# Combining the mean and variance of four token tiles on Pool, by nine small operations, instead of aggregating them on VectorE

## Chip, cores and metric

One core of one Trainium2 chip. The metric is the device time of one execution in microseconds (us). All runs told here are fast, with a mean granted clock of 0.99 to 1.0. A ratio is the mean time of one kernel's fast runs over the mean time of the other's fast runs of the same rounds, so it is not quite the ratio of the medians that stand beside it. Profiled executions are single ones; their span is 1.7 to 2.2 us shorter than the device time of the same execution.

## The reference, cut to what matters

```python
def _layernorm(x, axis=-1, eps=1e-05):
    m = jnp.mean(x, axis=axis, keepdims=True)
    v = jnp.var(x, axis=axis, keepdims=True)
    return (x - m) / jnp.sqrt(v + eps)
...
    # x: 2048 tokens x 512 channels, bf16
    h = _layernorm(x, axis=-1) * (1 + ca) + sa           # first norm
    x = x + ga * _A_ref(h, A_wqkv, A_wo)                 # windowed attention, 32 heads of 16
    h = _layernorm(x, axis=-1) * (1 + cb) + sb           # second norm
    x = x + gb * _B_ref(h, B_w1, B_b1, B_w2, B_b2)       # starts with a third norm, then mixes tokens
```

Tokens lie on the 128 partitions: 16 tiles of 128x512, handled in four sets of four. Three norms on four sets make twelve groups of statistics; each needs a mean and a reciprocal deviation for each of its four tiles.

## The kernel before

The sums (`bn_stats`) give, for each token, count, mean and sum of squared differences of the even channels and the same for the odd ones; the aggregation (`bn_aggr`) makes mean and variance of them. `ve`, `po`, `ac` and `te` are VectorE, Pool, ScalarE and TensorE. The whole kernel is one list of operations, and a table gives the order in which the engines get them.

```python
def e_stat(e, i):                                  # one tile: VectorE
    ...
    st = small.tile([P, nc.vector.BN_STATS_DIM], F32, name="st", tag=tag + "st")
    ve.bn_stats(out=st[:], in_=tiles(i)[:])
    ve.bn_aggr(out=box[box_key][0][:, i, :], in_=st[:])

def e_rs(e, a, b):                                 # four tiles: Pool (the other groups: ScalarE)
    mv, rs, _ = box[box_key]
    if e == "POOL":
        po.tensor_scalar(out=rs[:, a:b], in0=mv[:, a:b, 1], scalar1=EPS, scalar2=0.0, op0=ALU.add, op1=ALU.add)
        po.tensor_tensor(out=rs[:, a:b], in0=rs[:, a:b], in1=half_t[:, a:b], op=ALU.pow)
        return
    ...

def normalize(e, dst, src, key, i):                # xn or hb: waits for rs
    mv, rs, nm = box[key]
    if e == "DVE":
        ve.tensor_scalar(out=dst, in0=src, scalar1=mv[:, i, 0:1], scalar2=rs[:, i : i + 1], op0=ALU.subtract, op1=ALU.mult)
    else:
        po.tensor_scalar(out=dst, in0=src, scalar1=nm[:, i : i + 1], scalar2=rs[:, i : i + 1], op0=ALU.add, op1=ALU.mult)
```

(Cuts are marked by "...".) After the second norm comes `h = xn * bc`, `h = h + bc`, and the third norm makes `hb` of `h`. Beside the norms, ScalarE takes the exponentials of the attention (`et<-psa`, 75 of them of 128x1536), VectorE multiplies some of them by a mask (`et<-et,maskt`) and copies TensorE's results out of PSUM. (`QT`, `kb` and `VT` are queries, keys and values, `psa` and `psb` the scores in PSUM, `pxy` the products of exponentials and values, `pu` the products behind the third norm.)

The softmax here doesn't subtract the row's maximum and nothing guards it: scores larger than these inputs give would overflow.

Of the kernel before, what the change touches and what calls it, by code (L numbers as in the profile page):

```python
# [10 lines left out]
ALU = mybir.AluOpType  # L11
# [38 lines left out]
128 197 199 129D 328P 130A 99D 200 125D 154 71 126D 153 329D 201 110 72 73 207 111A 112D 208 113 74 198 115D 114D  # L50
202 181 182 203 155 183D 156 204 215 185 209 205 162 86 29 157D 216 163 789 30 206 210 165D 178 211 179 217 164D 223
212 166 224 213 184 167 180D 158 169D 159 168A 214 160D 218 225 161D 189 219 76 230 79 220 173 231 190 221 174 77
222 226 191D 175D 192 170 227 549 171 232 177 234 176 228 172D 186 235 187 193 229 194 330D 233 331D 332D 238 236
333D 334 188D 239 335 338 337D 339 237 336D 340D 246 240 341D 345 247 550 355 346 78 250 248 347D 356 251 349 241
357D 365 366 242 257 367D 252 389 258 790 350 390 243 261 259 244 351 262 245 352D 249 253 391D 265 254 551 392 263
373 266 75 359 374 87 370 375D 371 255 273 372D 267 342 274 552 381 382 256 343 383D 275 277 344D 385 260 278 264
348 360 268 358 279 395 361 396 353 287 362D 376 288 269 289 399 368 397 284 791 400 377 285 386 286 553P 387 270
403 401 271 792 364 272 404 276 369 280 388D 296 281 363 412 405 378 282 354 290 413 283 379 393 398 380D 394 554P
416 414 555P 297 402 417 384 406 291 556D 293 407 557D 423 418 292 558P 294 408 424 559 409 411 560 295 410 415 561D
425 428 298 419 429 562D 563 564 606 566D 420 432 565D 430 299 607 433 585 301D 300P 586 608D 421 587D 440 434 614  # L60
422 441 595 302D 596 303P 445 442 427 426 304D 793P 446 615 431 616D 452 447 597D 618 435 453 570 305P 571 444 436
306D 456 1034 454 572D 307P 1033 598 457 603 599 617 437 461 308P 458 438 604 314 462 309P 439 443 600D 448 605D 463
469 310P 449 590 470 591 580 311P 592D 450 473 589 471 451 581 315 474 460 455 573 459 312D 594 582D 481 475 567
794D 482 610 568 609 464 569D 465 485 316 602 483 575 486 593 611 576 601 466 489 487 583 467 577D 490 468 472 588
476 584 477 498 478 574 612 491 479 619 1032 613D 499 484 488 795D 313D 492 796P 317 493 502 500 509 480 797P 503
510 512 318P 513 494 620 504 495 798P 319D 621 496 511 501 321P 505 521 322P 506 626 514 622 518 507 320D 625 515
627 323P 508 516 623 497 578 522 631 628 579 519 517 632 520 624 629 640 633 523 799 641 803 800 804 524 634 645 642
525P 630 646 805D 635 526D 801D 527P 636 802D 653 647 806D 807 654 643 808 528D 810 809D 811 529P 637 658 655 812D
815 659 638 820 530D 816 648 531D 663 660 817D 639 664 644 661 649 532D 539 843 650 672 665 656 844 651 533D 673 821
652 534P 657 822D 666 677 674 662 678 535P 845D 854 540 667 668 536P 685 679 541 855 686 851 819 856D 852 537D 838  # L70
669 853D 538P 687 690 670 839 691 835 840D 836 675 695 692 680 671 688 696 676 693 681 837D 830 682 542 704 697 846
683 847 543P 705 684 831 698 689 544D 709 706 832D 547P 694 710 825 548D 813 699 848D 826 700 545D 717 711 546P 827D
1039 718 1040 707 1044 823 1041 701 722 712 719 1042 858 702 723 1045 1043D 841 703 708 814 727 724 1050 857 728 713
842 1046 714 736 833 729 1047 737 1051 828 1048D 1049 1052 859 1036 725 1053 715 818 741 1054D 738 752 742 720 753
849 716 749 721 730 743 860 824 726 754 861 731 744 1055 850 750 732 865 862 834 751 1056 866 1057 761 829 1061 1062
739 733 870 867 734 1058 762 871 735 1060 740 1059D 1035 745 1038 872 879 1063 746 873 880 1066 1067 868 1064 747
884 1065D 881 1068 748 885 1069 882 758 1071 1070D 759 1037 863 892 886 760 755 893 756 864 757 869 894 763 874 897
875 1072 898 764 1073 1074 895 765P 1077 887 876 899 902 877 1075 766D 903 767P 1078 1076D 878 768D 911 904 900 883
912 769D 888 770D 1079 771D 1083 889 772D 913 779 916 1084 917 1085 905 1086 1080 773D 890 918 924 1082 891 925 896
919 1081D 901 906 774D 914 907 929 1088 908 926 1089 909 775D 930 910 927 915 776P 780 920 921 934 777D 931 1087D  # L80
1090 778P 935 1091 781 1094 1095 1092D 922 943 782 936 988 944 1096 923 783P 1097 937 928 945 932 948 989 949 1098D
933 784D 990 938 787P 991 939 1000 950 786P 956 992 940 788P 957 1099 993 1100 785P 941 1101 1002 1102 1001 958 961
1104 1103D 1116 962 951 1117 1008 1119 946 1120 1003 1009 966 1118 963 942 947 967 1010 952 1121 1122 964 953 1105
1011 968 975 1012 954 1106 969 976 1123 1107 959 1108 955 1124 977 980 960 981 978 965 1109D 970 1125 1013 971 1110
1020 972 1126 982 973 1111 1021 983 974 1127 979 984 1022 994 985 1158 1172 1028 1112 986 1167 1113 1023 1093 987
1164 995 1029 1114A 1159 996 997 1160 998 1171 1004 1162 1128 1163 1129 999 1161 1005 1177 1115 1130 1131 1166 1132
1014 1168 1006 1134 1165 1189 1170 1015 1181 1007 1169 1133 1135 1016 1137 1136 1138 1017 1173 1139 1140 1201 1018
1024 1141 1185 1019 1143 1025 1026 1144 1142 1027 1030 1146 1031 1147 1145 1174 1178 1175 1190 1193 1176 1179 1205
1148 1180 1182 1186 1183 1202 1206 1187 1149 1188 1191 1194 1150 1184 1209 1192 1213 1195 1210 1151 1196 1197 1198
1152 1199 1153 1221 1200 1154 1222 1203 1155 1217 1204 1207 1156 1214 1157 1249 1211 1239 1240 1215 1259 1225 1216  # L90
1241 1208 1218 1229 1212 1219 1230 1260 1223 1242 1269 1231 1226 1261 1227 1232 1250 1228 1233 1224 1243 1279 1220
1299 1262 1234 1244 1289 1263 1251 1280 1252 1300 1253 1290 1254 1301 1255 1281 1235 1245 1236 1302 1282 1246 1283
1291 1256 1264 1247 1319 1309 1237 1284 1270 1238 1285 1271 1310 1292 1320 1311 1293 1312 1303 1272 1321 1322 1273
1265 1329 1266 1304 1274 1257 1275 1323 1276 1339 1313 1286 1330 1267 1349 1294 1268 1324 1258 1350 1248 1331 1332
1333 1325 1295 1340 1277 1341 1359 1296 1278 1334 1305 1297 1314 1287 1298 1360 1361 1306 1288 1315 1362 1316 1369
1351 1326 1335 1363 1317 1352 1327 1364 1342 1307 1343 1353 1336 1308 1370 1318 1344 1328 1345 1371 1346 1354 1379
1337 1355 1347 1372 1380 1356 1348 1365 1338 1373 1357 1374 1366 1358 1375 1381 1376 1382 1383 1377 1384 1367 1385
1386 1368 1378 1387 1388
# [55 lines left out]
def kernel(  # L154
# [357 lines left out]
    def norm_ops(tag, tiles, deps, poss, box_key, parts, pool=True):  # L512
        st_ops, rs_of = [], {}

# [9 lines left out]
        def e_stat(e, i):  # L524
            if i == 0:
                box[box_key] = (
                    small.tile([P, 4, nc.vector.BN_AGGR_DIM], F32, name="mv", tag=tag + "mv"),
                    small.tile([P, 4], F32, name="rs", tag=tag + "rs"),
                    small.tile([P, 4], F32, name="nm", tag=tag + "nm"),
                )  # L530
            st = small.tile([P, nc.vector.BN_STATS_DIM], F32, name="st", tag=tag + "st")
            ve.bn_stats(out=st[:], in_=tiles(i)[:])
            ve.bn_aggr(out=box[box_key][0][:, i, :], in_=st[:])

        def e_rs(e, a, b):
            mv, rs, _ = box[box_key]
            if e == "POOL":
                po.tensor_scalar(out=rs[:, a:b], in0=mv[:, a:b, 1], scalar1=EPS, scalar2=0.0, op0=ALU.add, op1=ALU.add)
                po.tensor_tensor(out=rs[:, a:b], in0=rs[:, a:b], in1=half_t[:, a:b], op=ALU.pow)
                return  # L540
            ac.activation(out=rs[:, a:b], in_=mv[:, a:b, 1], func=ACT.Ln, bias=eps_t[:], scale=1.0)
            ac.activation(out=rs[:, a:b], in_=rs[:, a:b], func=ACT.Exp, scale=-0.5)

        for i in range(4):
            prev = [st_ops[-1]] if st_ops else []
            st_ops.append(op(f"{tag}st", {"DVE": 0.82}, lambda e, i=i: e_stat(e, i), deps=deps[i] + prev, pos=poss[i]))
            for a, b in parts:
                if b == i + 1:
                    o = op(f"{tag}rs", {"ACT": 0.46, "POOL": 0.6 + 0.145 * (b - a)} if pool and tag != "l1" or b - a == 4 else {"ACT": 0.46}, lambda e, a=a, b=b: e_rs(e, a, b), deps=st_ops[:], pos=poss[i])
# [717 lines left out]
```

## Time and profile before

| | before |
|---|---|
| time, median (lowest to highest) | 267.67 us (267.42 to 267.75), 3 runs |
| span of the profiled execution | 265.2 us |
| ScalarE idle from 100 to 130 us | 0.06 us |
| first of the last long run of matmuls | 199.5 us |

The prediction below shows the lines that carry the reading. In the lines in the order in time come the start, the length, then the instruction; an idle time ahead of it stands in brackets. These three are the first instructions on VectorE that need the statistics of the groups at 107, 126 and 155 us:

```profile
110.03 0.41 DVE L194 TENSOR_TENSOR h<-xn,bc_all 128x512 bf16<-128x512 bf16 x1
...
128.47 0.57 DVE L194 TENSOR_SCALAR hb<-h,mv,rs 128x512 bf16<-128x512 bf16 x1
...
157.55 0.42 DVE L194 TENSOR_TENSOR h<-xn,bc_all 128x512 bf16<-128x512 bf16 x1
```

And this is the chain that ended last, by engine:

```profile
PE 67%; ACT 19%; DVE 8%; issue 4%; POOL 0%; ACTq 0%; POOLq 0%
```

Pool has no share in it.

### The profile page before, as it was taken

The numbers are of one execution on the slowest core, as the hardware profiler recorded it, in microseconds if no ns is written. First come the engines' busy times: TensorE is split into PE (matmuls) and PEld (weight loads), VectorE is DVE, ScalarE is ACT, GpSimd is POOL, SyncE is SP. The second block draws the span as 40 slices with busy tenths as digits, with TensorE's granted clock in tenths as the row PEclk, the third lists the DMA queues.
The fourth block names the chain that finished last, engine by engine and source line by source line (L and its number), as shares of the span: only waits on it lengthen the run. The fifth ranks groups of instructions, "written<-read, shape, count | busy, mean of one in ns | idle before, by whom it ended". The sixth has DMA issues, their size and how long they took to land.

```text
span 265.2 us, 10676 instructions
## 1 busy us (share of the span) xinstructions
PE 248.8 (94%) x4769; PEld 136.8 (52%) x4769; DVE 195.5 (74%) x444; ACT 185.4 (70%) x268; POOL 91.1 (34%) x153
## 2 busy tenths in 40 slices
PE   7898999999989888899999999999999999999993
PEld 2575666656656654455544454445444444444441
DVE  7768896777847559999948888999998730415875
ACT  2479999999999899999999999999416432000000
POOL 8054321495289946543893031440000000000000
PEclk9999999999999999999999999999999999999999
DMA  6996400000018000000015872011499800001122
GB/s 205 362 381 206 47 5 4 5 2 5 2 31 213 5 4 5 0 5 2 4 27 136 220 184 79 5 44 40 143 373 397 355 4 0 20 0 63 59 99 79
DMA packets 31598, 25.34 MB, mean 96 GB/s; under 512 B 6076, under 2 KB 29632, under 8 KB 31552
## 3 DMA queue, kind: packets, MB, share of 16 engines
q1 hardware_dynamic: 31544, 24.66, 29.5%
q8 instruction: 37, 0.61, 0.9%
q14 instruction: 9, 0.07, 0.1%
q10 hardware_dynamic: 8, 0.00, 0.0%
HBM read 22.55 MB, written 2.10 MB: 93 GB/s over the span
## 4 chain that ended last, share of the span: by engine, by line
PE 67%; ACT 19%; DVE 8%; issue 4%; POOL 0%; ACTq 0%; POOLq 0%
PE pu L194 32%; ACT et L194 16%; PE pxy L194 13%; PE psa L194 8%; PE pq L194 5%; PE pa L194 4%; PE pv L194 3%; ACT lz L194 3%; DVE st L194 2%; DVE VT L194 1%; PE pt L194 1%; DVE part L194 1%; PE psb L194 1%; DVE h L194 1%; DVE mv L194 0%
## 5 line engine op out<-in xcount | busy, mean ns | idle before, releaser
L194 ACT ACTIVATE et<-psa 128x1536 bf16<-128x1536 f32 x75 | 109.2, 1455 | 4.0 <-PE psa L194 1.9
L194 PE MATMUL pu<-hb,w1p 128*128 128x512 bf16 x224 | 53.2, 380 | 0.7 <-DVE part L194 0.7
L194 PE MATMUL pu<-guT,w 128*128 128x512 bf16 x224 | 49.0, 379 | 0.0
L194 ACT ACTIVATE et<-psb 128x512 bf16<-128x512 f32 x75 | 45.1, 601 | 0.0
L194 PE MATMUL pxy<-et,ones_bd 128*32 128x192 bf16 (+3 forms) x960 | 38.7, 233 | 0.7 <-issue 0.7
L194 PE MATMUL pxy<-et,VT 128*32 128x192 bf16 (+3 forms) x960 | 38.4, 234 | 0.9 <-DVE OT L194 0.5
L194 PEld LDWEIGHTS <-w 128*128 128x128 bf16 x224 | 21.9, 98 | 26.4
L194 PE MATMUL psa<-QT,KT 32*128 32x192 bf16 (+3 forms) x720 | 30.0, 230 | 5.6 <-ACT et L194 4.9
L194 POOL TENSOR_SCALAR KT<-kb,mask_par 128x512 bf16<-128x512 bf16 (+1 forms) x36 | 22.9, 645 | 31.0 <-DVE kb L194 22.3
L194 PEld LDWEIGHTS <-w1p 128*128 128x128 bf16 x224 | 20.2, 98 | 25.6 <-issue 2.3
L194 PE MATMUL pq<-h1T,wqkv 128*128 128x512 bf16 (+1 forms) x128 | 30.1, 355 | 0.3 <-ACT VT L194 0.3
L194 PEld LDWEIGHTS <-KT 32*128 32x128 bf16 x960 | 16.2, 92 | 26.4 <-issue 24.1
L194 PEld LDWEIGHTS <-VT 128*32 128x32 bf16 x960 | 23.6, 96 | 11.6 <-issue 10.1
L194 PE MATMUL psb<-QT,KT 32*128 32x192 bf16 (+3 forms) x240 | 29.4, 231 | 0.0
L194 DVE SCALAR_TENSOR_TENSOR o<-pu,b2FM,bc_all 128x512 f32<-128x512 f32 x16 | 11.6, 748 | 20.2 <-PE pu L194 20.1
L194 DVE TENSOR_TENSOR et<-et,maskt 128x512 bf16<-128x512 bf16 (+2 forms) x56 | 24.9, 480 | 0.6 <-ACT et L194 0.5
L194 PEld LDWEIGHTS <-ones_bd 128*32 128x32 bf16 x960 | 23.2, 97 | 1.0 <-issue 0.9
L194 DVE BATCH_NORM_STATS2 st<-x 128x6 f32<-128x512 bf16 x32 | 21.8, 680 | 0.2
L194 DVE TENSOR_TENSOR OT<-pxy,lz 128x256 bf16<-128x256 f32 x32 | 13.4, 419 | 10.6 <-ACT lz L194 10.1
L194 PEld LDWEIGHTS <-wqkv 128*128 128x128 bf16 x192 | 14.0, 97 | 13.4 <-issue 4.8
L194 PE MATMUL pv<-wqkv,h1T 128*32 128x256 bf16 x512 | 17.9, 274 | 0.2 <-DVE VT L194 0.2
L194 PE MATMUL pa<-wod,OT 128*128 128x512 bf16 x64 | 17.3, 381 | 0.3 <-ACT part L194 0.3
(113 smaller groups left out, 355.1 us busy)
## 6 DMA issues: line engine op xcount, KB each, us to landing
w1p<-in_B_w_dram SPq DMA_DIRECT2D x14, 512.0 KB, 6.3
w<-in_B_w_dram SPq DMA_DIRECT2D x14, 512.0 KB, 8.3
wmod<-in_w_mod_dram SPq DMA_DIRECT2D x6, 512.0 KB, 5.5
x<-in_A_x_dram SPq DMA_DIRECT2D x16, 128.0 KB, 4.6
out_dram<-otile SPq DMA_DIRECT2D x16, 128.0 KB, 1.7
wqkv<-in_A_wqkv_dram SPq DMA_DIRECT2D x2, 384.0 KB, 5.5
wqkv<-in_A_wqkv_dram SPq DMA_DIRECT2D x1, 512.0 KB, 5.3
wod<-in_A_wo_dram SPq DMA_DIRECT2D x1, 512.0 KB, 8.7
```

What stands on the lines that cost most here:

```text
L194: ins = call(*args, **kwargs)
```

## The change

The intent: VectorE is busy for 74% of the span and Pool for 34%, so Pool is to make mean and variance of four tiles at once, and VectorE keeps the sums only. It applies to nine of the twelve groups. The epsilon and the negated mean are folded into the nine operations, and the power follows. In the order of instructions each chain takes the place that the negated mean had.

```diff
 def e_stat(e, i):
+    if quad:                                       # the nine groups
+        if i == 0:
+            box[box_key, "st"] = small.tile([P, 4, nc.vector.BN_STATS_DIM], F32, name="st4", ...)
+        ve.bn_stats(out=box[box_key, "st"][:, i, :], in_=tiles(i)[:])
+        return
     st = small.tile(...)
     ve.bn_stats(out=st[:], in_=tiles(i)[:])
     ve.bn_aggr(out=box[box_key][0][:, i, :], in_=st[:])
+
+def e_agg(e):
+    t = small.tile([P, 4, 2], F32, name="agg", ...)
+    po.tensor_tensor(out=t[:, :, 0], in0=st[:, :, 1], in1=st[:, :, 4], op=ALU.subtract)
+    po.tensor_tensor(out=t[:, :, 1], in0=st[:, :, 1], in1=st[:, :, 4], op=ALU.add)
+    po.tensor_tensor(out=t[:, :, 0], in0=t[:, :, 0], in1=t[:, :, 0], op=ALU.mult)
+    po.tensor_scalar(out=mv[:, :, 0], in0=t[:, :, 1], scalar1=0.5, ...)
+    po.tensor_scalar(out=nm[:], in0=t[:, :, 1], scalar1=-0.5, ...)
+    po.tensor_scalar(out=t[:, :, 0], in0=t[:, :, 0], scalar1=0.25, scalar2=EPS, op0=ALU.mult, op1=ALU.add)
+    po.tensor_tensor(out=t[:, :, 1], in0=st[:, :, 2], in1=st[:, :, 5], op=ALU.add)
+    po.tensor_scalar(out=t[:, :, 1], in0=t[:, :, 1], scalar1=1.0 / D, ...)
+    po.tensor_tensor(out=mv[:, :, 1], in0=t[:, :, 0], in1=t[:, :, 1], op=ALU.add)

 def e_rs(e, a, b):
-    if e == "POOL":
-        po.tensor_scalar(out=rs[:, a:b], in0=mv[:, a:b, 1], scalar1=EPS, ...)
-        po.tensor_tensor(out=rs[:, a:b], in0=rs[:, a:b], in1=half_t[:, a:b], op=ALU.pow)
+    if quad:
+        po.tensor_tensor(out=rs[:], in0=mv[:, :, 1], in1=half_t[:], op=ALU.pow)
         return
```

## The prediction

> **What bounds the kernel now.** I read the page's busy shares first, then a table of busy time by stretch, then the groups that the change touches, then the order in time on Pool, VectorE and TensorE.
>
> ```profile
> PE 248.8 (94%) x4769; PEld 136.8 (52%) x4769; DVE 195.5 (74%) x444; ACT 185.4 (70%) x268; POOL 91.1 (34%) x153
> ```
>
> VectorE at 74% and Pool at 34% make the move look right: take from the busier, give to the idler. But 74% is a mean. By stretch (columns: stretch, its length, then the busy time of PE, PEld, DVE, ACT, POOL):
>
> ```profile
> 80.00:100.00 20.00, 18.10 (x647) 12.56 (x638) 12.13 (x27) 18.86 (x26) 15.97 (x25) 1.00 0.26 66
> 100.00:110.00 10.00, 7.75 (x169) 4.29 (x158) 9.84 (x24) 9.96 (x14) 6.07 (x10) 1.00 0.01 3
> 110.00:120.00 10.00, 9.47 (x269) 5.61 (x268) 9.68 (x23) 9.99 (x15) 5.07 (x5) 1.00 0.01 3
> 130.00:150.00 20.00, 20.00 (x379) 9.35 (x376) 14.19 (x29) 19.70 (x28) 11.49 (x15) 1.00 0.33 90
> 150.00:170.00 20.00, 19.43 (x425) 10.30 (x423) 17.91 (x45) 19.35 (x27) 4.27 (x5) 1.00 0.50 125
> 170.00:185.00 15.00, 15.00 (x305) 7.46 (x304) 14.24 (x35) 14.53 (x22) 4.90 (x6) 1.00 0.14 38
> 200.00:265.00 65.00, 60.96 (x283) 27.43 (x281) 33.71 (x52) 10.51 (x15) 0.00 (x0) 1.00 0.27 103
> ```
>
> From 100 to 120 us ScalarE (the exponentials) is busy 19.95 of 20 us and VectorE 19.52. From 130 TensorE is full, to 185 with ScalarE close behind; the last 65 us are TensorE alone. The chain that ended last says the same: PE 67%, ACT 19%, DVE 8%. So VectorE is nearly full from 100 to 130 and from 160 to 200, but beside another full engine. A shorter VectorE shortens the kernel only where a full engine waits for it, and those waits are small: from 40 to 185 us ScalarE's whole idle time is 4.2 us.
>
> **What the Trainium skill says.** "Perfetto Trace Analysis", section "Optimizing Scalar/DVE Operations": a VectorE instruction on SBUF has about 60 ns of access overhead that occupies the engine, its profiled latency being about twice that. The trace agrees in kind: the aggregation shows 182 ns, yet the next instruction starts 0.10 us after it. The section also warns that moving work between VectorE and Pool may not help as they share a port. "SBUF — State Buffer", section "SBUF: two separate sides": that shared pair is an exclusive lock, held for a whole instruction, against Pool's reads, by VectorE instructions in a two-port mode or with two SBUF inputs. The mask multiply has two SBUF inputs, and the trace agrees: a Pool scalar operation on 128x4 takes 0.23 to 0.24 us alone and 0.85 beside a mask multiply. "GPSIMD Engine Reference", section "Instruction dispatch": each Pool instruction passes a sequencer and a software dispatcher, so small size doesn't make it cheap; here 128x4 takes about what a 64x64 copy takes (233 ns).
>
> **The change part by part.** It touches nine of the twelve groups of statistics (three norms on four sets of tiles); the first set of the first norm and the last set of the other two keep the old way.
>
> ```profile
> L194 DVE BATCH_NORM_AGGREGATE mv<-st 128x2 f32<-128x6 f32 x48 | 8.7, 182 | 1.7
> L194 DVE SCALAR_TENSOR_TENSOR nm<-mv 128x4 f32<-128x4 f32 x8 | 1.4, 180 | 0.1
> L194 POOL TENSOR_SCALAR rs<-mv 128x4 f32<-128x4 f32 x9 | 3.0, 337 | 32.5 <-DVE mv L194 32.4
> L194 POOL TENSOR_TENSOR rs<-rs,half_t 128x4 f32<-128x4 f32 x9 | 9.9, 1104 | 0.8
> ```
>
> VectorE loses 36 of 48 aggregations and the eight 128x4 negated means. An aggregation costs its slot: sums plus aggregation take 0.82 us start to start (49.58 to 50.40), a copy of the sums' duration 0.61 (50.84 to 51.45), so about 0.21. 36 x 0.21 + 8 x 0.09 = 8.3 us of slots, about 8 us off the busy time of 195.5.
>
> Pool gains nine small operations per group and loses the addition of epsilon and the one negated mean it had. At 0.235 us: 81 x 0.235 - 3.0 - 0.2 = +15.8, so Pool's busy time goes to about 107 us (40%), somewhat more with lock waits.
>
> The latency is what matters. In the built program seven of the ten operations wait for one before them on Pool. Such a pair costs 0.33 us start to start (56.29 to 56.62), operations that do not wait 0.20 (eight copies in 1.56). Two at 0.20 and seven at 0.33 give 2.7, plus the power of 1.03: 3.7 us from the last sum to the reciprocal deviation, against 0.33 + 1.03 = 1.36 now. The aggregation off VectorE gives 0.2 back: about 2.1 us later per group, 3 where mask multiplies hold the lock. Order: each chain now stands where the negated mean stood; nothing else in the order of PE, ACT or the queues changes. On VectorE later instructions that need the statistics then block what stands behind them.
>
> Pool, VectorE and TensorE around the two groups that matter most:
>
> ```profile
> 106.81 0.85 POOL L194 TENSOR_SCALAR rs<-mv 128x4 f32<-128x4 f32 x1 [2.87 <-DVE mv L194]
> 107.74 1.03 POOL L194 TENSOR_TENSOR rs<-rs,half_t 128x4 f32<-128x4 f32 x1
> 108.88 0.76 POOL L194 TENSOR_SCALAR xn<-x,nm,rs 128x512 bf16<-128x512 bf16 x1
> ...
> 170.24 0.23 POOL L194 TENSOR_SCALAR rs<-mv 128x4 f32<-128x4 f32 x1 [1.66 <-DVE mv L194]
> 170.56 1.65 POOL L194 TENSOR_TENSOR rs<-rs,half_t 128x4 f32<-128x4 f32 x1
> 172.71 3.02 POOL L194 TENSOR_SCALAR hb<-h,nm,rs 128x512 bf16<-128x512 bf16 x4 [0.50 <-DVE nm L194]
> ```
>
> ```profile
> 110.03 0.41 DVE L194 TENSOR_TENSOR h<-xn,bc_all 128x512 bf16<-128x512 bf16 x1
> ```
>
> ```profile
> 174.47 1.89 PE L194 MATMUL pu<-hb,w1p 128*128 128x512 bf16 x8
> 176.63 1.90 PE L194 MATMUL pu<-hb,w1p 128*128 128x512 bf16 x8
> ```
>
> Group by group, in time:
> - 20 us: the first consumer is at 34.8. Nothing.
> - 61 us: normalized tiles about 2 us later, transposes at 65.5 and 67.9. Just fits.
> - 70 us: VectorE's normalize at 72.06 waits until about 73.4; the copies behind it come some 0.5 us later. Cost 0 to 0.5.
> - 74 us: moves to about 86, into Pool's stretch without a gap (75.6 to 93.4), and delays keys, values and the small copies that free exponential buffers by 3.5 to 4 us. The first exponential of the next group of tiles starts at 98.84; those are ready at 95 to 96.5. Just fits.
> - 97 us: statistics at 101.5 instead of 98.3; VectorE's first `hb` (101.11) stalls about 1 us. Cost 0 to 1.
> - 107 us: beside mask multiplies, so 3.7 to 4.3 us; Pool's normalize ends near 111, while VectorE wants it (the row at 110.03) and would by then be there a little earlier. A stall of 1 to 2 us with ScalarE and VectorE both full. Cost 0.5 to 1.
> - 126 us: `hb` of the sixth tile on Pool goes from 130.45 to about 132; its first matmul is the eighth from 130.27, at 131.8. Cost 0.3 to 0.8, TensorE being full.
> - 155 us: VectorE stalls about 1.5 us at 157.55 in front of mask multiplies. Cost 0.3 to 1.
> - 170 us: Pool makes all four `hb`, the last at 175.7; the matmuls at 176.63 start with that last one. Spare 0.9, delay 0.2 to 1.2 after VectorE's own gain of 0.6. Cost 0 to 0.5.
>
> Sum of costs 1.1 to 4.8, middle about 2.5. Against it stands VectorE's gain: of 8.3 us most falls in gaps or beside full engines. I give it 1 to 1.5 us, for matmuls and exponentials that now wait for an evacuation or a mask. Net about +1.2, so 268.9 us.
>
> **Rivals.**
> (1) VectorE is a real bound from 100 to 130 and from 160 to 200; its 8 us count in part, and the time falls by 1 to 3 us (265 to 266.5). For it: 98% busy from 100 to 110. Against it: ScalarE at 99.6% there, TensorE at 100% from 170 to 185, and the last 10 us before the final matmuls (189.7 to 199.5), the one VectorE-led stretch of the chain, holds only tiles that the change leaves alone.
> (2) Pool's chains stall VectorE's queue at five places; the stalls spread, since TensorE runs in order and the score banks leave it about 0.2 us per chunk before ScalarE waits. All 4.8 us and the locks: 272 to 274. For it: Pool was without a gap from 75.6 to 93.4. Against it: six exponential buffers and TensorE's idle 2.25 us from 100 to 110.
> (3) All delays are absorbed and nothing gained: 267.5, the same.
>
> **Range and chances.** My middle is between (2) and (3): 268.9, range 266.4 to 272.2. Two per cent is 5.35 us: below 262.3 nothing in the trace leads, as ScalarE's and TensorE's work is unchanged: 0.03. Above 273.0 needs rival (2) almost whole: 0.10. The rest, 0.87, within 2%.
>
> **What would show it.** Right, if in the changed profile VectorE's busy time is 187 to 188, Pool's 105 to 110, each chain from first small operation to the end of the power is 3.5 to 4.5 us, VectorE shows new waits for Pool near 72, 101, 110 and 157 of 0.5 to 2 us, and the final matmuls start 0 to 3 us later than 199.5. Wrong, if these matmuls start before 198.5 (VectorE was a bound), or if ScalarE's idle time between 100 and 130 goes from 0.1 to over 3 us (stalls spread), or if a small Pool operation takes over 0.4 us on average.

## The result and the profile after

| | before | after |
|---|---|---|
| time, median (lowest to highest) | 267.71 us (267.42 to 268.0), 4 runs | 271.09 us (270.64 to 271.44), 4 runs |
| ratio, 95% interval | | 1.0125 (1.0107 to 1.0144) |
| span of the profiled execution | 265.2 us | 268.9 us |
| first of the last long run of matmuls | 199.5 us | 203.2 us |

The kernel is slower by 3.4 us. That lies in the predicted range of 266.4 to 272.2, but the loss is nearly three times the +1.2 us that the prediction gave.

The busy times on the page after:

```profile
PE 244.9 (91%) x4727; PEld 136.8 (51%) x4769; DVE 189.7 (71%) x400; ACT 185.8 (69%) x268; POOL 105.8 (39%) x224
...
PE 56%; DVE 14%; POOL 12%; ACT 11%; issue 5%; POOLq 0%; ACTq 0%
```

VectorE lost 5.8 us and Pool gained 14.7, as planned, and the chain that ended last (the second line) now goes over Pool for 12%, where it had 0%. (42 matmul records are missing in this trace, x4727 for x4769, so TensorE's busy time can't be compared to a per cent.) Pool's new work, from the groups of instructions (count, then busy time and mean ns, then idle time before and what ended it):

```profile
L193 POOL TENSOR_TENSOR rs<-mv,half_t 128x4 f32<-128x4 f32 x9 | 9.4, 1050 | 0.7
L193 POOL TENSOR_TENSOR agg<-st 128x4 f32<-128x4 f32 x27 | 6.0, 240 | 24.7 <-DVE st L193 24.0
L193 POOL TENSOR_SCALAR agg<-agg 128x4 f32<-128x4 f32 x18 | 4.2, 232 | 1.5
```

The same stretches as in the prediction (busy time of PE, PEld, DVE, ACT and POOL, then the granted clock, the DMA share and GB/s):

```profile
100.00:110.00 10.00, 6.95 (x157) 3.93 (x156) 9.06 (x19) 9.29 (x14) 7.73 (x18) 1.00 0.01 3
110.00:120.00 10.00, 8.54 (x238) 5.16 (x241) 8.25 (x19) 9.17 (x12) 5.18 (x5) 1.00 0.01 3
130.00:150.00 20.00, 18.63 (x420) 9.52 (x414) 12.96 (x26) 18.48 (x26) 14.92 (x19) 1.00 0.22 59
150.00:170.00 20.00, 18.36 (x389) 9.77 (x394) 16.06 (x37) 18.59 (x25) 4.69 (x12) 1.00 0.59 156
170.00:185.00 15.00, 14.14 (x276) 6.96 (x271) 13.81 (x32) 14.59 (x24) 7.77 (x15) 1.00 0.13 37
```

ScalarE, which was busy for 19.95 of the 20 us from 100 to 120, is now busy for 18.46; from 130 to 150 it has lost 1.2 us. No engine is full any more: the engines wait for each other. Pool around the group at 107 us shows how:

```profile
106.63 1.00 POOL L193 TENSOR_TENSOR agg<-st 128x4 f32<-128x4 f32 x2 [1.75 <-DVE st L193]
107.58 0.20 POOL L193 TENSOR_TENSOR agg<-agg 128x4 f32<-128x4 f32 x1
...
108.75 0.20 POOL L193 TENSOR_SCALAR agg<-agg 128x4 f32<-128x4 f32 x1
109.03 0.20 POOL L193 TENSOR_TENSOR mv<-agg 128x4 f32<-128x4 f32 x1
109.31 1.31 POOL L193 TENSOR_TENSOR rs<-mv,half_t 128x4 f32<-128x4 f32 x1
110.73 0.77 POOL L193 TENSOR_SCALAR xn<-x,nm,rs 128x512 bf16<-128x512 bf16 x1
```

One small operation that waits for the one before it comes 0.28 us after it (108.75, 109.03) and takes 0.20. The chain from the first operation to the end of the power takes 3.99 us here (106.63 to 110.62), where the kernel before took 1.96 (106.81 to 108.77, in the prediction's lines). Where no mask multiply is near it takes 3.06 (the groups at 20 and 97 us). On VectorE, the three instructions of the last section are now these:

```profile
111.53 0.42 DVE L193 TENSOR_TENSOR h<-xn,bc_all 128x512 bf16<-128x512 bf16 x1 [1.78 <-POOL xn L193]
...
131.17 0.41 DVE L193 TENSOR_SCALAR hb<-h,mv,rs 128x512 bf16<-128x512 bf16 x1 [1.44 <-POOL rs L193]
...
161.61 0.42 DVE L193 TENSOR_TENSOR h<-xn,bc_all 128x512 bf16<-128x512 bf16 x1 [1.39 <-POOL xn L193]
```

All three wait for Pool. Behind each of them stand copies that TensorE needs, and behind TensorE stand the exponentials:

```profile
104.93 0.29 PE L193 MATMUL pxy<-et,VT 128*32 128x256 bf16 x4 [1.01 <-POOL VT L193]
112.61 1.66 PE L193 MATMUL pv<-wqkv,h1T 128*32 128x256 bf16 x48 [0.90 <-DVE QT L193]
132.24 1.73 PE L193 MATMUL pu<-hb,w1p 128*128 128x512 bf16 x6 [0.65 <-DVE kb L193]
```

```profile
114.65 1.45 ACT L193 ACTIVATE et<-psa 128x1536 bf16<-128x1536 f32 x1 [0.83 <-PE psa L193]
```

This suggests a ruler for all that follows: number the 75 exponentials of 128x1536, and take the start of each in the changed kernel minus its start in the kernel before. This *slip* grows only where time is lost. For the changed kernel it is -0.26 at the first (17.7 us), -0.25 at the 35th (96.7 us) and +3.70 at the last (183.6 us), and it grows in six steps. I number the nine groups by their time in the kernel before: 1 at 20 us, 2 at 61, 3 at 70, 4 at 74 (moved to 86), 5 at 97, 6 at 107, 7 at 126, 8 at 155, 9 at 170.

| step of the slip | near | follows from | size, us |
|---|---|---|---|
| groups 1, 2, 3 | to 80 us | | 0 |
| groups 4 and 5 | 105 us | TensorE waits for Pool's values (`VT`, started at 103.52 for 102.60) | 0.67 |
| group 6 | 113 us | VectorE's `h` waits for Pool | 0.82 |
| group 7 | 132 us | VectorE's `hb` waits for Pool | 1.09 |
| group 7, second step | 141 us | | 0.25 |
| group 8 | 165 us | VectorE's `h` waits for Pool | 0.83 |
| group 9 | 179 to 181 us | TensorE waits for Pool's `hb` | 0.29 |
| sum from the 35th exponential on | | | 3.95 |

The ruler has an error that has nothing to do with the change. The slip of the first exponential differs from profile to profile by up to 2.2 us (it is 0.33 us in one kernel below that is as fast as the kernel before). TensorE also has pauses that the profile puts down to "issue", near 87 us (0.70 us before, 1.03 after) and sometimes near 159 us, and they too differ from profile to profile. So I read steps at the groups, not the slip as a whole. The step of 0.67 us at groups 4 and 5 came only with both of them changed: with groups 1 to 4 alone, and with 5, 7 and 9 alone (both below), no step stands near 105 us.

### The profile page after: what moved, and what is told of

Its sections match the earlier page's. It is cut to its first block, busy times and chain, and to the rows that moved or that the text cites. A ratio compares the mean times of both kernels' runs of the same rounds, so it can differ in the third digit from the quotient of the medians.

```text
span 268.9 us, 10666 instructions
## 1 busy us (share of the span) xinstructions
PE 244.9 (91%) x4727; PEld 136.8 (51%) x4769; DVE 189.7 (71%) x400; ACT 185.8 (69%) x268; POOL 105.8 (39%) x224
## 4 chain that ended last, share of the span: by engine, by line
PE 56%; DVE 14%; POOL 12%; ACT 11%; issue 5%; POOLq 0%; ACTq 0%
PE pu L193 29%; ACT et L193 9%; PE pxy L193 7%; PE psa L193 6%; PE pq L193 6%; PE pv L193 4%; DVE st L193 3%; POOL agg L193 3%; PE pa L193 2%; DVE et L193 2%; POOL rs L193 2%; ACT lz L193 2%; POOL hb L193 2%; DVE h L193 1%; DVE part L193 1%
## 5 line engine op out<-in xcount | busy, mean ns | idle before, releaser
L193 PE MATMUL pu<-hb,w1p 128*128 128x512 bf16 x212 | 51.8, 380 | 2.6 <-DVE kb L193 0.7
L193 PEld LDWEIGHTS <-KT 32*128 32x128 bf16 x960 | 15.6, 92 | 25.8 <-issue 23.8
L193 PE MATMUL pq<-h1T,wqkv 128*128 128x512 bf16 (+1 forms) x112 | 27.4, 350 | 1.4 <-issue 0.8
L193 POOL TENSOR_SCALAR VT<-vn,half_m 128x512 bf16<-128x512 bf16 x24 | 17.8, 755 | 0.0
```

What stands on the lines that cost most here:

```text
L193: ins = call(*args, **kwargs)
```

## The experiments

The theory: the loss is how late the reciprocal deviations come, which the engines pass on one to one where nothing hides it; the work taken off VectorE earns nothing by itself. Rivals: (a) the load on Pool and on the port that it shares with VectorE slows both; (b) the new place in the order of instructions costs; (c) VectorE's relief earns its few microseconds and hides an even larger loss.

### Relief without lateness, lateness without relief, order, a shorter chain

**Relief alone.** The kernel before, with the aggregations dropped from the nine groups; mean and variance are read from the even channels' sums. The statistics are wrong, though the result was still within the tolerance.

```diff
-    ve.bn_aggr(out=box[box_key][0][:, i, :], in_=st[:])
+    # nine groups: mv is the view st[:, :, 1:3] (mean and squares of the even channels)
-    po.tensor_scalar(out=rs, in0=mv[..1], scalar1=EPS, scalar2=0.0, op0=ALU.add, op1=ALU.add)
+    po.tensor_scalar(out=rs, in0=mv[..1], scalar1=2.0 / D, scalar2=EPS, op0=ALU.mult, op1=ALU.add)
```

> The kernel before with the 36 aggregations simply left out of VectorE (the mean and spread are read from the even half alone, so the result is wrong on purpose); Pool does what it did before, in the order of before. Theory 'late statistics' (the loss comes from statistics that arrive later, VectorE's relief is worth little): 266.9 to 267.6, final matmuls at most 0.5 to 0.8 us earlier. Rival 'VectorE is a bound in two stretches': 263 to 265.5.

Measured: 268.28 us beside 267.13, ratio 1.0041 (1.0023 to 1.006): slower than the 266.9 to 267.6 expected, and far from the rival's 263 to 265.5. VectorE's busy time fell to 190.5 us and the reciprocal deviations came 0.11 to 0.45 us earlier, and nothing was gained: from the 35th exponential on no step of the slip is below -0.01 us. The small loss consists of 0.57 us ahead of the first exponential, of pauses of TensorE by "issue" (1.30 us near 87, 0.52 near 160) and of 0.33 us near 119. There VectorE's mask multiply took 1.81 us in place of 0.95, and TensorE waited 0.48 us for it. It had started (118.09) behind a Pool multiply of 1.16 us that was running (117.93). In the kernel before VectorE was first (117.21, Pool 117.25), and Pool's multiply took 1.93 us. So which of the two comes first decides who loses there.

**Lateness without relief.** The changed kernel, with the 36 aggregations put back on VectorE, into tiles that nobody reads.

```diff
     ve.bn_stats(out=box[box_key, "st"][:, i, :], in_=tiles(i)[:])
+    spare = small.tile([P, nc.vector.BN_AGGR_DIM], F32, name="spare", tag="spare")
+    ve.bn_aggr(out=spare[:], in_=box[box_key, "st"][:, i, :])
     return
```

> The kernel after with the 36 aggregations kept on VectorE as well, their results unread: the Pool chains without the relief. Late statistics: 271.3 to 272.3, because the relief showed only as 0.4 us of earlier exponentials before 80 us. Rival 'VectorE is a bound': 273 or more, as the relief then hid part of the delay.

Measured: 273.02 us beside 267.13, ratio 1.0238 (1.0211 to 1.0264). The theory's 271.3 to 272.3 failed, and the rival's 273 or more came true: beside late chains the relief is worth 2.5 us by the medians (5.9 lost here, 3.4 by the changed kernel, on different chips). From the 35th exponential on the steps sum to 4.5 us here and to 3.95 in the changed kernel, so only 0.55 of the 2.5 us can be placed at the groups. The two profiled executions differ by 1.8 us, and 1.2 of it lies ahead of 88 us. Of that, 0.37 is there at the first `pq` matmul (9.85 us for 9.48), ahead of the first aggregation put back (15.74), and 0.35 is a wait of TensorE for the DMA of a weight near 14 us, so these are not the aggregations' doing. What makes up the rest of the 2.5 us stays open, and rival (c) is not out by this run.

**Order alone.** The kernel before, with its two Pool operations moved to where the changed kernel has its chain.

```diff
-... 301D 300P ...        # reciprocal deviation ahead of its old place
+... 301D ... 300P ...    # at the place that the changed kernel gives it, nine times
```

> The kernel before, with only the place of Pool's two operations (epsilon, power) moved behind the negated mean, as in the kernel after. Late statistics: 267.4 to 268.3, the same as before. Rival 'the place in the order': most of the loss, 269.5 to 271.

Measured: 267.29 us beside 267.13, ratio 1.0001 (0.9981 to 1.0021). Rival (b) is out.

**Six operations for nine.** Correct too: the sums are added pairwise in one operation of 128x8, the negated mean is made of that, and VectorE's normalize adds it.

```diff
-    (nine operations)
+    po.tensor_tensor(out=t[:], in0=st[:, :, 1:3], in1=st[:, :, 4:6], op=ALU.add)
+    po.tensor_scalar(out=nm[:], in0=t[:, :, 0], scalar1=-0.5, ...)
+    po.tensor_scalar(out=t[:, :, 1], in0=t[:, :, 1], scalar1=1.0 / D, scalar2=EPS, ...)
+    po.tensor_tensor(out=t[:, :, 0], in0=st[:, :, 1], in1=nm[:], op=ALU.add)
+    po.tensor_tensor(out=t[:, :, 0], in0=t[:, :, 0], in1=t[:, :, 0], op=ALU.mult)
+    po.tensor_tensor(out=mv[:, :, 1], in0=t[:, :, 0], in1=t[:, :, 1], op=ALU.add)
```

> The kernel after with six small operations in place of nine (both sums in one operation, half the difference as even mean plus negated mean, the mean read by VectorE as the negated mean): right result. Chain without lock waits about 2.2 us in place of 3.06. Late statistics: a loss about in proportion to the time over the 1.36 us of before, so 268.8 to 269.8; rival 'place in the order' or a loss that only one large wait makes: 270.5 to 271.

Measured: 269.01 us beside 267.13, ratio 1.0069 (1.0053 to 1.0086). As expected: three operations fewer take back about half of the loss.

### Which groups

The changed kernel's code in some groups and the old code in the others:

```diff
-quad = parts == [(0, 4)]
+quad = parts == [(0, 4)] and box_key in QUADS     # groups 1 to 4; 5, 7 and 9; 6 and 8
```

> The change in the first four groups only (20, 61, 70 and 74 us), the other five as before. In the trace of the kernel after, the exponentials slip by no more than about 0.3 us against before until the fifth group. Late statistics: 267.0 to 267.8. Rival 'Pool backlog' (the fourth chain, moved into the stretch without a gap, delays keys and values of the next tiles): 0.7 us or more of loss, 267.8 to 268.8.

> The change in groups five, seven and nine only (97, 126 and 170 us: the third norm). From the slips of the exponentials in the kernel after (0.67 at 104, 1.1 at 133, 0.3 at 180) late statistics gives +2.1, less where the fifth no longer meets the backlog of the fourth: 268.4 to 269.4. Rival 'only the order or the sum counts': a third of the loss, 268.2.

> The change in groups six and eight only (107 and 155 us: second norm, VectorE waits for Pool's normalized tile). Slips in the kernel after 0.82 and 0.83: late statistics 268.4 to 269.1. Rival: two ninths of the loss, 267.9.

Measured, beside 266.98 us:

| groups changed | median | ratio, 95% interval | steps of the slip |
|---|---|---|---|
| 1 to 4 | 267.45 us | 1.0013 (0.9999 to 1.0027) | none at the groups |
| 5, 7, 9 | 269.66 us | 1.0095 (1.0079 to 1.0111) | group 7: 1.53 and 0.25; group 9: 0.34 |
| 6, 8 | 269.54 us | 1.0092 (1.0078 to 1.0105) | group 6: 1.28; group 8: 1.17 |

The first four groups are free, as expected. (The second kernel has two more steps of 0.3 us: near 96, where TensorE had paused by "issue" for 0.33 us, and near 119, where the mask multiply took 1.81 us as under "Relief alone".) The other two sets cost somewhat more than expected, and together more than all nine at once: group 6 steps by 1.28 us here and by 0.82 in the changed kernel. There 0.67 us were already lost at groups 4 and 5, and lateness counts from what is lost already.

### Load or lateness

**Fillers ahead of the wait, in all groups.** The kernel before, and ahead of each addition of epsilon seven small operations in a chain that nobody reads. Pool carries the load, and in its idle time, if it has any there.

```diff
+    fill = small.tile([P, 4, 2], F32, name="fill", ...)
+    po.tensor_tensor(out=fill[:, :, 0], in0=half_t[:], in1=half_t[:], op=ALU.add)
+    for n in range(6):
+        po.tensor_scalar(out=fill[:, :, (n + 1) % 2], in0=fill[:, :, n % 2], scalar1=0.5, scalar2=0.0, op0=ALU.mult, op1=ALU.add)
     po.tensor_scalar(out=rs[:, a:b], in0=mv[:, a:b, 1], scalar1=EPS, ...)
     po.tensor_tensor(out=rs[:, a:b], in0=rs[:, a:b], in1=half_t[:, a:b], op=ALU.pow)
```

> The kernel before with seven small dependent operations that nobody reads put on Pool in front of each of the nine additions of epsilon. They need nothing from VectorE, so where Pool would have idled for the statistics they run in the idle time: nearly the load of the kernel after on Pool and on the shared port, without later statistics. Late statistics: 267.0 to 268.0 (the fourth group, in Pool's stretch without a gap, may cost up to 0.8). Rivals 'Pool's load' and 'port contention': 269 to 271.

Measured: 269.58 us beside 266.98, ratio 1.0098 (1.008 to 1.0115). The expectation failed, and by itself this looks like rival (a). But the slip is 2.94 us by the 31st exponential (87.6 us) and 2.95 at the 52nd (132.6 us): the fillers of groups 5 and 6 and the first step of group 7 cost nothing (0.55 us near 141 us is all that follows), and the loss lies ahead of them, at groups 1 to 4. Not all of it need be the fillers': in this profile TensorE's granted clock was 0.50 from 81.4 to 84.8 us, where it was 1.0 in the kernel before. Up to 1.7 us of the 2.94 (half of these 3.4, an estimate) can be that. At groups 1, 2 and 4 Pool does not wait ahead of the addition (at group 3 it waits 6.59 us). In the kernel before, around group 4:

```profile
73.80 0.46 POOL L194 TENSOR_SCALAR rs<-mv 128x4 f32<-128x4 f32 x1
...
76.33 0.76 POOL L194 TENSOR_SCALAR xn<-x,nm,rs 128x512 bf16<-128x512 bf16 x1
```

and with the fillers:

```profile
75.34 1.58 POOL L194 TENSOR_SCALAR fill<-fill 128x4 f32<-128x4 f32 x6
76.99 0.24 POOL L194 TENSOR_SCALAR rs<-mv 128x4 f32<-128x4 f32 x1
...
79.02 0.77 POOL L194 TENSOR_SCALAR xn<-x,nm,rs 128x512 bf16<-128x512 bf16 x1
```

No idle time stands ahead of the addition there, so the fillers made the statistics late, and with them everything behind them on Pool, which the experiment was meant not to do; load and lateness can't be told apart in these groups. (The changed kernel avoids that, since it moves this chain to 86 us.) So the next pair was made for groups 5 to 9 only.

**The same fillers ahead of the wait, or behind it.** In the first kernel the seven operations stand ahead of the addition of epsilon, in the second between it and the power. The two kernels have the same instructions.

```diff
-                (all groups)
+                if box_key in LATE:          # groups 5 to 9
                     fill ... seven operations, ahead of the addition
```

> Groups 5 to 9 only: seven small operations that nobody reads, in a chain, on Pool ahead of the addition of epsilon, where Pool waits for the sums anyway. Pool carries the load of the change, its port use is there, but no statistic is later by more than a few tenths. Theory (the loss is how late the statistics are): within 0.4 us of the kernel before, 266.7 to 267.4. Rival (Pool's load and the shared port slow VectorE): 268 to 269.5, with mask multiplies slower than before. The earlier run with fillers in all groups lost 2.4 us ahead of 90 us; if the theory holds that part is gone here.

```diff
                 po.tensor_scalar(out=rs[:, a:b], in0=mv[:, a:b, 1], scalar1=EPS, ...)
+                if box_key in LATE:
+                    fill ... the same seven operations
                 po.tensor_tensor(out=rs[:, a:b], in0=rs[:, a:b], in1=half_t[:, a:b], op=ALU.pow)
```

> The same seven operations in the same five groups, but between the addition of epsilon and the power, so that every reciprocal deviation comes about 1.8 us later (more beside mask multiplies). VectorE keeps its aggregations. Theory: the loss of the changed kernel without its relief, 269.8 to 271.5, with new stalls at exponentials 42, 51 and 66. Rival (load): the same as the run with the operations ahead of the addition.

Measured, beside 267.06 us on one chip: ahead 267.13 us, ratio 1.0002 (0.9982 to 1.0022); behind 272.97 us, ratio 1.0214 (1.0193 to 1.0234). On VectorE, the three instructions with the fillers ahead:

```profile
110.06 0.41 DVE L196 TENSOR_TENSOR h<-xn,bc_all 128x512 bf16<-128x512 bf16 x1
...
128.49 0.58 DVE L196 TENSOR_SCALAR hb<-h,mv,rs 128x512 bf16<-128x512 bf16 x1
...
157.82 0.43 DVE L196 TENSOR_TENSOR h<-xn,bc_all 128x512 bf16<-128x512 bf16 x1 [0.17 <-POOL xn L196]
```

and with the same fillers behind:

```profile
111.93 0.43 DVE L196 TENSOR_TENSOR h<-xn,bc_all 128x512 bf16<-128x512 bf16 x1 [1.95 <-POOL xn L196]
...
131.97 0.41 DVE L196 TENSOR_SCALAR hb<-h,mv,rs 128x512 bf16<-128x512 bf16 x1 [1.78 <-POOL rs L196]
...
162.71 0.43 DVE L196 TENSOR_TENSOR h<-xn,bc_all 128x512 bf16<-128x512 bf16 x1 [1.75 <-POOL xn L196]
```

Pool's busy time is 99.0 us in the one and 99.3 in the other, both 8 above the kernel before. In the first every step of the slip from the 35th exponential on is 0.02 us or less; in the second they sum to 5.5 us. In these groups the load costs nothing that the runs can show (the interval ends at 1.0022), and the lateness costs all. Rival (a) is out here, by the cleanest pair. The second kernel lost more than I expected (269.8 to 271.5): I had sized it from the changed kernel, whose chains in groups 6 to 8 are less late (table below).

**A chain shorter than before.** The addition of epsilon is dropped, so the power reads the variance (the result stays within tolerance).

```diff
-    po.tensor_scalar(out=rs[:, a:b], in0=mv[:, a:b, 1], scalar1=EPS, scalar2=0.0, op0=ALU.add, op1=ALU.add)
-    po.tensor_tensor(out=rs[:, a:b], in0=rs[:, a:b], in1=half_t[:, a:b], op=ALU.pow)
+    po.tensor_tensor(out=rs[:, a:b], in0=mv[:, a:b, 1], in1=half_t[:, a:b], op=ALU.pow)
```

> The kernel before without the addition of epsilon (the power reads the variance itself; the result is still within tolerance): each chain is 0.33 us shorter, up to 0.9 beside mask multiplies, in all nine groups. If the kernel before already waits for these chains, the time falls by 0.2 to 1 us; if it has slack there, by under 0.2 us: 266.8 to 267.0. The theory says that the kernel before waits 1.0 us for Pool's normalized tile in group 6 and hardly elsewhere, so 0.2 to 0.6 us faster.

Measured: 267.12 us beside 267.06, ratio 1.001 (0.9985 to 1.0034). Reciprocal deviations 0.34 to 0.95 us earlier in groups 5 to 9 earn nothing. The expectation of 0.2 to 0.6 us failed: it put VectorE's wait of 1.0 us for a normalized tile into group 6, while it lies at 77 us, in another group. The kernel before isn't short of statistics anywhere, so it isn't one end of a straight line: it has slack.

### How much slack

For each kernel I took how much later than in the kernel before VectorE starts its first instruction that needs the statistics, less the slip that was already there ahead of the group, and set against it the step of the slip that follows. An entry is "late / step", in us; a dash is a group that the kernel leaves as it was.

| kernel | group 6 | group 7 | group 8 |
|---|---|---|---|
| fillers ahead, groups 5 to 9 | 0.02 / 0.00 | 0.01 / 0.00 | 0.26 / 0.00 |
| two fillers behind (below) | 0.57 / 0.31 | 0.50 / 0.12 | 0.45 / 0.00 |
| six operations | 0.60 / 0.34 | 1.16 / 0.78 | 0.99 / 0.33 |
| the changed kernel | 1.08 / 0.82 | 1.46 / 1.09 | 1.48 / 0.83 |
| the same with aggregations kept | 1.53 / 1.26 | 1.47 / 1.10 | 1.75 / 1.30 |
| groups 6 and 8 | 1.54 / 1.28 | - | 1.61 / 1.16 |
| groups 5, 7 and 9 | - | 1.90 / 1.53 | - |
| seven fillers behind | 1.73 / 1.47 | 1.86 / 1.49 | 1.84 / 1.39 |
| **late minus step, where there is a step** | **0.26 to 0.27** | **0.37 to 0.38** | **0.45, or 0.65 to 0.66** |

The difference is the same to 0.01 us in kernels whose losses differ by more than four times. Each group has a fixed slack, and past it every 0.1 us late is 0.1 us lost. (By itself this says that the path from VectorE's instruction to the exponential is then the one that ends last; that late statistics feed it is shown by the pair above.) In group 8 the larger value is that of the two kernels in which group 9 has lost its aggregations: one of those (at 160.73 us before) stands between VectorE's `h` and the mask multiplies behind it, and its slot is the 0.21 us that the prediction read for an aggregation. In the trace the last sums and the mask multiply behind them start 0.82 us apart with it (160.01 and 160.83) and 0.60 without (164.07 and 164.67 in the changed kernel). That fits the 0.20; no run takes out this one aggregation alone.

**A test of the slack.** Two fillers behind the addition, in place of seven.

```diff
-    fill ... seven operations
+    po.tensor_tensor(out=fill[:, :, 0], in0=half_t[:], in1=half_t[:], op=ALU.add)
+    po.tensor_scalar(out=fill[:, :, 1], in0=fill[:, :, 0], scalar1=0.5, scalar2=0.0, op0=ALU.mult, op1=ALU.add)
```

> As the run with seven operations between the addition of epsilon and the power in groups 5 to 9, but with two of them: every reciprocal deviation about 0.48 us later. From the earlier runs each group has a slack that must be used up first, read as lateness minus step: 0.61 us in group 6, 1.00 in group 7, about 0.44 in group 8 (with the aggregations on VectorE), 1.24 in group 9. Theory: steps of the exponentials of 0 at groups 5, 6, 7 and 9 and 0.05 at group 8, so no loss: 266.7 to 267.5 beside a kernel before of 267.1. Rival (no slack, each 0.1 us costs its share): 0.48 of 1.8 us of the 5.5 us that seven operations cost, so +1.4 us, 268.5.

(The slacks in this text, 0.61, 1.00 and 1.24 us, were counted from the end of the power on Pool; the table counts from VectorE's instruction, which is the better place, since Pool's own normalize lies between and can be held up.) Measured: 268.97 us beside 267.12, ratio 1.0056 (1.0035 to 1.0076). The time missed the expectation, and lies nearer to the rival's 268.5; the trace tells two causes apart. First, the steps from the 35th exponential on are 0.31, 0.12, 0.19 (the second step of group 7), 0.00 at group 8 and 0.00 at group 9: 0.6 us in all. Two fillers gave more lateness than the 0.48 us that I counted on where a mask multiply ran: in group 7 one of them took 0.94 us in place of 0.20, and in group 6 Pool's normalize behind the power took 1.28 in place of 0.76.

```profile
129.68 0.94 POOL L196 TENSOR_SCALAR fill<-fill 128x4 f32<-128x4 f32 x1
```

With the lateness that they really had, the slack holds in all three groups, and groups 8 and 9 did get later for nothing. Second, this profile, the slowest of the six runs (267.81 to 270.35 us), starts its first exponential 2.2 us late: TensorE waited 0.32 us for the DMA of a weight near 14 us, and its granted clock was 0.50 from 15.5 to 18.9 us (four matmuls in 1.06 us for 0.60). That does not explain the median: the other five runs had a mean clock of 0.996 to 1.0 (this one 0.993), and those at 1.0 took 268.02 and 268.85 us. Of the median's 1.85 us some 1.2 stay open. So the slack is shown in the steps, and not in the total, which does not rule out the rival's 268.5.

Two more ways to shorten the old chain, the addition and the power as one operation on VectorE or on Pool, did not build. No kernel beats the kernel before; with the change in groups 1 to 4 only, and with the fillers ahead in groups 5 to 9, it is the same.

## Why the prediction was right or wrong

The picture was right: VectorE's 74% is no bound, its relief is no gain of its own, Pool's chains are late where VectorE's queue needs them, and the time comes out 0 to 2% slower. The sizes were not. The prediction summed the groups' costs to "1.1 to 4.8, middle about 2.5", and took off a gain of "1 to 1.5 us".

| step as predicted | predicted | shown |
|---|---|---|
| VectorE's busy time | 187 to 188 us | 189.7 |
| Pool's busy time | 105 to 110 us | 105.8 |
| one small operation | under 0.4 us, some 0.235 | 0.232 on average (81) |
| chain, first operation to the end of the power | 3.5 to 4.5 us | 3.06 alone, 3.34 to 3.99 beside mask multiplies |
| groups at 20, 61, 70 us | 0, 0, 0 to 0.5 us | 0 |
| groups at 74 and 97 us | 0, and 0 to 1 | 0.67 together |
| group at 107 us | 0.5 to 1 | 0.82 |
| group at 126 us | 0.3 to 0.8 | 1.34 |
| group at 155 us | 0.3 to 1 | 0.83 |
| group at 170 us | 0 to 0.5 | 0.29 |
| costs together | 1.1 to 4.8, middle 2.5 | 3.95, relief included; 4.5 without it |
| VectorE's gain | 1 to 1.5 | none alone; beside late chains 0.55 of those 4.5 at the groups, 2.5 by the medians |
| final matmuls later | 0 to 3 us | 3.7 |
| ScalarE's idle time, 100 to 130 | not over 3 us | 1.55 |

**The step that failed is the sum.** Of the costs with a range, the group at 70 us came at the low end (0), four came in the upper half, and the group at 126 us came above its range: 1.34 for 0.3 to 0.8. (The middle of 1.1 to 4.8 is also 2.95, not the 2.5 that was carried on.) At 126 us the prediction followed Pool's `hb` of the sixth tile to the eighth matmul, and passed over VectorE's own `hb` (128.47 us), which stands ahead of a copy of keys (`kb`) that TensorE waits for. It had written that "later instructions that need the statistics then block what stands behind them" and did not apply it there. Of the four places named for new waits on VectorE, those near 72, 110 and 157 us came (1.07, 1.78 and 1.39 us); near 101 none came, as VectorE came to its `hb` (100.56) just as the power that it needs ended (100.53), and one came at 131 us that was not named. One error went the other way: the chain was put at 3.7 us alone, with links of 0.33 and 0.20 read from other pairs of operations. Its own took 0.28 (five of them) and 0.16, so it was 3.06.

**The gain was taken off twice.** Inside the groups the prediction had VectorE "there a little earlier" at 107 us and took off "VectorE's own gain of 0.6" at 170; then it took off 1 to 1.5 us once more. The steps show where the relief acts: at group 8 (late by 1.48 us with it and 1.75 without, and 0.2 us more slack) and at group 9 (0.29 us for 0.47). Groups 4 to 6 together lose the same with it and without (1.49 and 1.46 us). That is inside the costs. Outside them relief alone earned nothing (ratio 1.0041); beside late chains the medians say 2.5 us, of which no more than this is placed, so the size of the gain there stays open. With 3.95 (relief included) for 2.5 and nothing more for 1.25, the +1.2 becomes +3.95; the changed kernel's profile shows 3.70 us, and the medians 3.4.

Of the rivals, (1) is refuted by the relief alone. The mechanism of (2), stalls that spread, is the right one, with steps that pass on one to one past the slack; its size, 4.8 us and more, was not reached, since slack and relief take something back. (3) holds for groups 1 to 4 taken alone (ratio 1.0013), and not for the later ones.

The Trainium skill's page "Perfetto Trace Analysis", section "Optimizing Scalar/DVE Operations", warns that moving work between VectorE and GPSIMD might not help because of their shared port. Here it didn't help, but the port is the lesser part of it: the same small operations, ahead of the wait, cost 0.0% (1.0002), and behind it 2.1%. What the port did is lengthen single links of the chain, which fits the exclusive lock of the page "SBUF — State Buffer", section "SBUF: two separate sides": a small operation took 0.78 to 1.00 us for 0.20 beside a mask multiply of 128x1536, and the multiply itself 1.81 for 0.95 where Pool was first.

## What to carry to other kernels

Before moving work to an idle engine, find the first instruction in another engine's queue that needs the result, and how long it could come later before the full engine behind it starves: lateness below that slack is free, and past it is lost one to one. Don't credit a shorter busy time on an engine that no full engine waits for; what could be placed of it here was less lateness and more slack, which the costs held already. Before reading one profile's slip, look at its granted clock stretch by stretch. To tell load from lateness, put the same dummy operations once ahead of the wait and once behind it, and check in the trace that the engine really was waiting there.

## What the Trainium skill lacked or had wrong

- "GPSIMD Engine Reference", section "Instruction dispatch", describes the dispatch steps of an instruction but gives no total for a tiny elementwise one. Here a 128x4 operation on Pool takes 0.20 us, follows one that it depends on by 0.28 us from start to start, and a power of 128x4 takes 1.01 to 1.05 us at most places (up to 1.65).
- "SBUF — State Buffer", section "SBUF: two separate sides", states the exclusive lock but no figure for what it does to tiny Pool operations (its measured case is a DMA): 0.20 us became 0.78 to 1.00 us beside a mask multiply of 128x1536, and a normalize of 128x512 went from 0.76 to 1.28 us. It hit one link of a chain, not all of them.
- "Perfetto Trace Analysis", section "Optimizing Scalar/DVE Operations", gives the shared port as the reason why moving work between VectorE and GPSIMD may not help. Here the main reason was the length of the chain on the path: the same operations cost nothing ahead of the wait (ratio 1.0002) and 2.1% behind it (1.0214).
- No page I read covers TensorE's pauses that the profile puts down to "issue": 0.57 to 1.30 us near 87 us in 13 of the 14 traces (0.33 near 84 us in the other, the one with fillers in all groups), whatever the kernel.
